# Attention and a layer of four experts on one core: rows of two groups loaded as 512-byte runs and regrouped, first weights in smaller parts, gate rows in steps, a new order

## The chip, the core and the metric

The kernel runs on one core of one Trainium2 chip. The metric is the device time of one execution in microseconds (us), and lower is better. The core has a matrix engine (TensorE, PE in the profile, with its weight loads as PEld), a vector engine (DVE), a scalar engine (ACT), a general engine (POOL) and one that issues transfers (SP). They work beside each other and wait for one another by semaphores. In this kernel POOL, SP and, for the first rows, ACT issue the transfers (DMAs).

## The reference

Sliding-window attention with four sink keys goes into a layer of four experts, whose outputs are mixed by normalized gates:

```python
batch, n_heads, seq, head_dim = (4, 8, 768, 64);  n_sink, window = (4, 128)
scores = scale * np.matmul(q, k.transpose(0, 1, 3, 2))
rel = pos[:, None] - pos[None, :]
keep = (pos[None, :] < n_sink) | ((rel >= 0) & (rel < window))
scores = np.where(keep, scores, -1000000000.0)
a = np.exp(scores - scores.max(-1)); a = a / (a.sum(-1) + 1e-09)
x = np.matmul(a, v)          # heads side by side: x is [3072, 512]
p = domain_probs / (domain_probs.sum(-1, keepdims=True) + 1e-09)
for e in range(4):           # w1[e] is [512, 1024], w2[e] is [1024, 512]
    h = np.maximum(x @ w1[e], 0.0)
    out += p[:, e:e + 1] * (h @ w2[e])
```

The inputs are fp32; the kernel computes in bf16 with fp32 sums.

## The kernel before, in words

**Tiling.** A batch has 768 tokens, taken as six row blocks of 128, and two row blocks are a *group* of 256 tokens (`g` is 0, 1, 2: groups one, two and three). Eight heads of 64 are four *head pairs* (`hp`) of 128 columns. For each group and head pair the kernel computes scores (L702), exponentials (ACT, L728, one for each of the two heads `ph`), the values product (L762 for the sink keys, L769 for the rest, with a column of ones that gives the denominator), the reciprocal (DVE, L796) and the normalized product, which is `x`, turned so that its columns lie on the partitions. For each group and expert there is then a first layer with w1 and a second layer with w2.

**Batch 0 differs from batches 1 to 3.** In batch 0 rows are loaded to SBUF and turned by TensorE (L596 in `transposes`, called a *flip*); the result lies in PSUM and is copied to `qkT` by ACT and DVE (L295 in `copy`; for group one two copies of 256 columns for a head pair, for the others one of 512 on either engine). Its `x` is normalized by DVE (L799) and turned by TensorE (L828, `turn`). In the other batches DMAs that transpose, issued by SP, do both (L270 in `turn_nat`, L786).

**The first rows.** `load_first` (L280) brings q and k of group one, half of the heads at a time, from SP's and ACT's queues in fp32, each partition with two neighbouring tokens, so that a run in DRAM is 512 bytes. `cast_first` (L301) turns them into bf16, one copy of 512 columns on DVE for q and one on ACT for k for each half. Groups two and three come by `load_nat` (L247): a DMA of 128 KB (in bf16) on POOL for each row block and each of q and k, which casts on the way; a run is one token of one head, 64 values, 256 bytes in DRAM and 128 bytes in SBUF.

**POOL's queue at the start.** In this order: values of row blocks 0 and 1 (`load_v`, L322), rows of group two (four loads), values of 2 and 3, w1 of expert 0 in two halves of its columns (`load_w1`, L332; 512 KB each as it lands in bf16), w2 of expert 0 as one (`load_w2`, L345; 1 MB). Behind it the loop issues the rows of group three (four loads), values of 4 and 5, then w1 and w2 of experts 1 and 2; w1 and w2 of expert 3 and all of batch 1 follow when the attention of batch 0 has been issued.

**Masks.** From an upper triangle made by a scan on DVE come two bias matrices `low` (two of the steps on ACT), and from these two masks (L543). In group one of batch 0 TensorE adds `low` to the scores by a product with the identity (L696); in the other groups of batch 0, and in all of batches 1 to 3, DVE multiplies the exponentials by the mask (L721, L737).

**First layer.** Two forms exist. The plain one (`hps`, L1081) makes four pairs of 128 hidden columns (`QF`), each 8 products of 256 columns, for one group and expert. The fast one (`cps`, L1169) does with seven half-size block products what takes eight otherwise; it needs sums of blocks of w1 (`vf`, DVE, L404 and its neighbours in `weight_form1`) and of `x` (`T`, DVE, L1138 in `tokens`), and DVE and ACT combine its results. If its second bank was last used by a tile that isn't a whole bank, one product of 512 columns sets the bank first (L1177). **Second layer.** In batch 0 it is plain (L1411): for each row block and expert 8 products of 512 columns, then a scaling by the gate into `osb` (ACT for expert 0, L1421, and DVE adds for the others, L1427). In batches 1 to 3 it is done by seven products too (`acc`, L1343), on sums of blocks of w2 (`wf`, `weight_form`).

**Gates.** For batch 0 the gates are turned by four small transposes (L931 in `gates`), just ahead of the first second-layer product. For the other batches `gates_by_row` (L457) normalizes all gate rows in four DVE steps (L458 to L462), SP writes them to DRAM, and `load_gate` (L479) spreads each over the partitions.

**Order.** There is no scheduler at run time: when the program is built, a planner walks along TensorE's clock. It keeps a modelled time for each engine and queue (`t`), for each load when it lands (`lands`, `sp`), and for each operand when it is ready. At every step it lists what TensorE could do next (an attention step, a product of the first layer, one of the second layer, one of `acc`), sorts by readiness and priority, and takes the first, or another where the table `OTHER` says so for that numbered choice. Work for ACT and DVE is put down by `later(engine, ready, slack, run)` and issued by `flush` when the modelled clock passes; "any" goes to the engine that is free sooner by the model. When nothing is ready early on, it issues idle products on zeros (`idle_products`, L572), 9 of 512 columns at the start and more of 256 where there is a gap. The numbers at the head of the function (`LOW_PRODUCT`, `DUE`, `MARGIN` and so on) weigh these choices.

Of the kernel before, what the change touches and what calls it, by code (L numbers as in the profile page):

```python
# [8 lines left out]
AF = mybir.ActivationFunctionType  # L9
# [7 lines left out]
def kernel(  # L17
# [12 lines left out]
    nc = tc.nc  # L30
# [28 lines left out]

    HELD = ("unit", "early")  # L60
    NGATE = 5
    ANYLAG = (-40.93, 0.0, 0.0, 51.99)
    OTHER = {31: 1, 83: 1, 70: 1, 73: 1, 106: 1, 189: 1, 149: 1, 182: 2, 132: 1, 90: 1, 164: 1, 318: 1, 197: 1, 569: 2, 56: 3, 61: 1, 12: 1, 62: 1, 5: 1, 15: 3, 71: 1, 84: 1, 107: 2, 165: 2, 151: 1, 95: 1, 86: 1, 173: 1, 152: 1, 155: 3, 279: 1, 235: 1, 266: 1, 316: 1, 381: 3, 379: 1, 194: 1, 343: 1, 283: 3, 273: 1, 325: 1, 328: 1, 267: 1, 482: 1, 499: 2, 571: 1, 396: 1, 564: 3, 496: 1}
    TOKENS0 = 0.0
# [3 lines left out]
    SHARE_OF = (1.034, 1.037, 1.072)  # L68
    LEAD = (1.027, 0.9932)
    DUE = (1.356, 1.635, 1.356, 1.356)  # L70
    LOW_PRODUCT = (2.147, 2.149, 2.147, 2.147)
    LOW_SECOND = (2.509, 2.509, 3.0, 2.509)
    HIGH_PRODUCT = -1
    EARLY = (0.1973, 0.1973, 0.1973, 0.1973)
    MASK_SLACK = (200.0, 984.1, 200.0, 200.0)
    GATE = (2639.0, 2639.0, 2639.0, 2639.0)
    GATE0 = (6000.0, 6000.0, 6000.0, 6000.0)
    FORM = (1000.0, 1000.0, 1000.0, 1000.0)
    TOKEN = (4927.0, 4559.0, 4924.0, 4559.0)
    MARGIN = (4621.0, 2117.0, 2117.0, 2117.0)  # L80
    HOLD = 0
    FULL = (8, 8, 9, 9)
    STEP0 = (0.2923, 0.1633, 0.2843, 0.2923)
# [12 lines left out]
    LOADN = 0  # L96
    BIASED = 1
# [8 lines left out]
    t = {"pe": 1200.0, "act": 0.0, "dve": 0.0, "pool": 1280.0, "sp": 800.0, "sw": 4800.0, "hw": 0.0}  # L106
# [5 lines left out]
    WARM = 6600.0  # L112
    FLIP, LATE = 103.6, 618.6
# [82 lines left out]
    ROW = {64: 12.8, 128: 22.6, 512: 79.8, 1024: 156.2}  # L196

    def lands(key, rows, cols, *deps):
        issued = pool(0, *deps, fixed=880)
        at = max(t["sw"], issued + 1500)  # L200
        t["sw"] = at + rows * ROW[cols] / 16
        landed[key] = t["sw"] + 900 + (BACKLOG if key[0] == "w1" or backed else 0.0)
        if key[0] == "w1":
            backed.append(key)
        moved.append([key, at, t["sw"], ROW[cols]])

    moved, backed = [], []
    BACKLOG = 1300.0
    TURNED, SHARE = 66, 31.0

    def sp(*deps, issue=530, takes=600, turning=False):
        t["sp"] = max([t["sp"], *deps]) + issue
        at = max(t["hw"], t["sp"] + 800)
        row = next((x[3] for x in moved if x[1] <= at < x[2]), 0.0)
        if turning and row:
            t["hw"] = at + TURNED * (row + SHARE)
            t["sw"] += TURNED * SHARE
            for x in moved:
                if x[2] > at:
                    x[1] += TURNED * SHARE * (x[1] > at)  # L220
                    x[2] += TURNED * SHARE
                    landed[x[0]] = x[2] + 900 + BACKLOG * bool(backed)
                    if x[0][0] == "w1" and ("w1", x[0][1]) in landed:
                        landed["w1", x[0][1]] = max(landed["w1", x[0][1]], landed[x[0]])
        else:
            t["hw"] = at + takes + max(0.0, min(takes, t["sw"] - at)) * (not turning)
        return t["hw"] + 900
# [38 lines left out]
    def turn_nat(b, tb):  # L266
# [7 lines left out]
        turned_at[b, tb] = sp(landed["qk", b, tb], scored_at.get(b - 1, 0.0), issue=1330, takes=1400, turning=True) + LATE  # L274
# [4 lines left out]

    def load_first():  # L280

        raw = {name: mo.tile([P, 2, 4, 2 * D], FP32, name=f"{name}raw", tag=f"wide{i}", bufs=1) for i, name in enumerate("qk")}
        for half in range(2):
            hs = slice(4 * half, 4 * half + 4)
            for name, src in (("q", q), ("k", k)):
                x = raw[name][:, half]
                (nc.sync if name == "q" else nc.scalar).dma_start(
                    out=x, in_=src[0, hs, 0:G, :].rearrange("h (p t) d -> p h (t d)", t=2),
                )
                nat[0, half, name, "raw"] = x  # L290
            landed["first", half] = ((4870.0, 5180.0), (7550.0, 7350.0))[half]
            t["sp"] += 530
# [4 lines left out]
    first = {name: sb.tile([P, 2, H, D], BF16, name="qkn", tag="qkn", bufs=NQB) for name in "qk"}  # L297
    qkn_free[-2:] = [1e12] * 2
    cast_at = {}

    def cast_first(half):  # L301
        hs = slice(4 * half, 4 * half + 4)

        def cast(at):
            cast_at[half] = at

        part = join(2, cast)
        for i, name in enumerate("qk"):
            def run(engine, i=i, name=name):
                copy(  # L310
                    engine, first[name][:, :, hs, :],
                    nat[0, half, name, "raw"].rearrange("p h (t d) -> p t h d", t=2),
                )
                part(clock(engine, 512))
            later(("dve", "act")[i], landed["first", half][i], 0, run)

    def rows_at(b, g):
        return max(landed.get(("qk", b, tb), 1e12) for tb in (2 * g, 2 * g + 1))
# [26 lines left out]
    def load_w2(e):  # L345
        w2_sb[e] = wpool.tile([P, NFB, Dout], BF16, name=f"w2_{e}", tag=f"w2_{e}")
        nc.gpsimd.dma_start(out=w2_sb[e], in_=moe_w2[e].rearrange("(fb p) d -> p fb d", p=P))
        lands(("w2", e), F, Dout)
# [104 lines left out]
    identf = scratch[:, 9 * P:10 * P]  # L453
    nc.sync.dma_start(out=dp, in_=moe_domain_probs.rearrange("(tb p) e -> tb p e", p=P))
# [3 lines left out]
    def gates_by_row():  # L458
        nc.vector.reduce_sum(out=ds, in_=dp, axis=AX.X)
        nc.vector.tensor_scalar_add(out=ds, in0=ds, scalar1=1e-9)  # L460
        nc.vector.reciprocal(out=ds, in_=ds)
        nc.vector.tensor_mul(  # L462
            pn, dp.rearrange("n p e -> n e p"), ds[:, None, :].to_broadcast([NT, E, P]),
        )
        for i in range(2):
            nc.sync.dma_start(out=gate_rows[:, :, i, :], in_=pn[i:NT:2])
        dve(1800, 0.0)

    gate_sb = {}

    def load_gates():

        while len(gate_sb) < len(mix.order) and (
            len(gate_sb) < NGATE or mix.order[len(gate_sb) - NGATE] in mix.finished
        ):
            b, g, e = mix.order[len(gate_sb)]
            load_gate(b * NG + g, e)

    def load_gate(pair, e):  # L479
# [6 lines left out]
        sp(takes=300)  # L486


    held = consts.tile([P, 2], BF16, name="held")
    nc.vector.memset(identf, 1.0)  # L490
    lent = wpool.tile([P, 12 * P], BF16, name="lent", tag=f"wf_{E - 2}")
    zeros = lent[:, 0:4 * P]
    nc.vector.memset(zeros, 0.0)
# [3 lines left out]
    for h in range(H):  # L497
        r = 32 * (h // 2) + NSINK * (h % 2)
        nc.sync.dma_start(
            out=vsf[r:r + NSINK, :, 0:D], in_=v[:, h, 0:NSINK, :].rearrange("b j d -> j b d"),  # L500
        )
    ident = consts.tile([P, P], BF16, name="ident")
    for sgn in (1, -1):
        nc.gpsimd.affine_select(
            out=identf, in_=identf, compare_op=ALU.is_ge, fill=0.0,
# [5 lines left out]
    t["sw"] += 500  # L511
    for tb in (2, 3):
        load_nat(0, tb)
    load_v(0, (2, 3))
    load_w1(0, 2, [0])
    load_w1(0, 2, [1])
    t["sw"] += 700
    load_w2(0)

    nc.vector.tensor_copy(out=ident, in_=identf)  # L520
    nc.vector.reduce_sum(
        out=sel2, in_=identf.rearrange("p (h x j) -> p h x j", h=NHP, j=NSINK)[:, :, 0:2], axis=AX.X,
    )
    own = lent[:, 4 * P:5 * P]
    nc.vector.tensor_tensor_scan(own, ident, ident, 0.0, ALU.add, ALU.max)
    two = own[:, None, :].to_broadcast([P, 2, P])
    LOW = 32768.0
    low = [lent[:, 5 * P:8 * P], lent[:, 8 * P:12 * P]]
    nc.vector.tensor_scalar(
        out=low[0].rearrange("p (n q) -> p n q", n=3)[:, 0::2], in0=two, scalar1=LOW, scalar2=-LOW, op0=ALU.mult, op1=ALU.add,  # L530
    )
    nc.vector.tensor_scalar(out=low[0][:, P:2 * P], in0=own, scalar1=-LOW, scalar2=None, op0=ALU.mult)
    nc.vector.memset(low[0][0:NSINK, 0:2 * P], 0.0)
    x = low[1].rearrange("p (n c q) -> p n c q", n=2, c=2)
    nc.scalar.activation(out=x[:, :, 0], in_=two, func=AF.Copy, scale=-LOW)
    nc.scalar.activation(out=x[:, :, 1], in_=two, func=AF.Copy, scale=LOW, bias=-LOW)
# [4 lines left out]
    def make_mask(i):  # L541
        def run(engine):
            x = (mask0, mask1)[i]  # L543
            nc.vector.tensor_scalar(out=x, in0=low[i], scalar1=1 / LOW, scalar2=1.0, op0=ALU.mult, op1=ALU.add)
            dve(4 * P)
            made.append(i)
        later("dve", 9500.0, 5000, run)

    for i in range(2):
        make_mask(i)  # L550
    t["dve"] = t["act"] = 4600.0
    cast_first(0)
    flush(4700.0)
    for x in vx:
        nc.vector.memset(x[:, :, D:DX], 1.0)
    t["dve"] += 240.0
# [10 lines left out]
    t["dve"] += 400.0  # L567
    cast_first(1)

# [1021 lines left out]
```

## Time and profile before

| | |
|---|---|
| time, median of 3 runs | 360.43 us (359.46 to 360.57) |
| the profiled execution, whole | 359.9 us |
| its span, first to last instruction | 358.0 us |
| TensorE busy, whole span | 350.0 us |
| DVE, ACT, POOL busy | 294.7, 169.0, 69.7 us |
| granted TensorE clock, mean | 1.00 |
| moved by DMAs | 37.25 MB, 104 GB/s on average |

The span begins with the first instruction and ends with the last; 1.9 us of the profiled execution lie outside it. Busy times of engines overlap and don't add up to the span. The page gives them for the whole span; the trace gives the same by stretches, by line of the kernel, by tile, and as waits, each with what ended it. In a row of such a view stand the start in us from the span's beginning, the length, engine, line, operation, and the operands as out<-in, with partitions x elements; `xN` is a count of neighbouring instructions of one kind, and what stands in brackets is idle time ahead and what ended it. "DMA share" is the mean busy share of the core's 16 DMA engines.

### The profile page before, as it was taken

Reading aid. Unit: us, or ns where it says so; the run is one execution under the profiler, and the core shown is the slowest. Engines: PE = TensorE matmul, PEld = TensorE weight load, DVE = VectorE, ACT = ScalarE, POOL = GpSimd, SP = SyncE. Lnnn points to the kernel's source line nnn. Section 1 sums busy time; section 2 is a strip of 40 time slices with the busy share of each in tenths; the row PEclk is TensorE's granted clock in tenths of the full one; section 3 lists DMA queues with packets and bytes.
Section 4 is the critical chain, followed back from the end, with each engine's and each line's share of the span. In section 5 each row is a group of like instructions: output and inputs, shape, how many; then the busy total and the mean of one; then the engine's idle time right before and its main releaser. Section 6 shows DMA issues by size and latency. Waiting matters only on the chain.

```text
span 358.0 us, 10605 instructions
## 1 busy us (share of the span) xinstructions
PE 350.0 (98%) x4457; PEld 296.5 (83%) x4470; DVE 294.7 (82%) x625; ACT 169.0 (47%) x425; POOL 69.7 (19%) x90
## 2 busy tenths in 40 slices
PE   8799999999999999999999999999999999999996
PEld 3484867766668888898999799899999999999985
DVE  6753999878948799899799789989989899897750
ACT  5775735557844555466455564655321313312110
POOL 8935116123910860010020000000000000000000
PEclk9999999999999999999999999999999999999999
DMA  9999999999999997618990141512102002100021
GB/s 172 182 187 200 210 210 176 147 145 174 154 169 214 173 178 66 99 47 101 168 160 19 32 79 42 60 60 60 34 16 90 26 22 78 29 31 31 2 73 46
DMA packets 117291, 37.25 MB, mean 104 GB/s; under 512 B 100612, under 2 KB 112740, under 8 KB 117244
## 3 DMA queue, kind: packets, MB, share of 16 engines
q0 software_dynamic: 77520, 17.31, 53.3%
q1 hardware_dynamic: 38668, 18.75, 26.4%
q8 instruction: 35, 0.57, 0.7%
q10 hardware_dynamic: 1056, 0.52, 0.6%
q14 instruction: 12, 0.10, 0.1%
HBM read 40.45 MB, written 9.49 MB: 139 GB/s over the span
## 4 chain that ended last, share of the span: by engine, by line
PE 83%; DMA 6%; DVE 4%; ACT 2%; POOL 2%; issue 2%; SPq 0%; DVEq 0%; POOLq 0%
PE cps L1169 32%; PE acc L1343 31%; PE acc L1411 8%; PE hps L1081 5%; DMA xT<-onat 2%; PE sps L702 2%; PE od L769 2%; DMA qkn<-in_k_dram 2%; DMA rows<-in_k_dram 1%; ACT aT L728 1%; DMA qkT<-rows 1%; DVE aT L721 1%; DVE osb L1427 1%; PE od L762 1%; POOL qkn L258 1%
## 5 line engine op out<-in xcount | busy, mean ns | idle before, releaser
L1169 PEld LDWEIGHTS <-w 128*128 128x128 bf16 x1248 | 77.3, 98 | 4.3 <-issue 2.0
L1343 PEld LDWEIGHTS <-H 128*128 128x128 bf16 x600 | 55.9, 98 | 5.9 <-issue 0.5
L1202 DVE SCALAR_TENSOR_TENSOR H<-cps,gates 128x512 bf16<-128x512 f32 x84 | 57.2, 684 | 3.1 <-PE cps L1169 1.3
L728 ACT ACTIVATE aT<-sps 128x512 bf16<-128x512 f32 (+1 forms) x96 | 47.2, 575 | 19.0 <-PE sps L702 18.9
L1169 PEld LDWEIGHTS <-vf 128*128 128x128 bf16 x768 | 47.5, 98 | 1.7 <-issue 0.2
L1343 PE MATMUL acc<-w,H 128*128 128x256 bf16 x360 | 48.8, 273 | 0.0
L1169 PE MATMUL cps<-T,w 128*128 128x128 bf16 x624 | 47.3, 219 | 0.2 <-DVE H L1237 0.2
L1169 PE MATMUL cps<-xT,w 128*128 128x128 bf16 x624 | 47.1, 219 | 0.0
L808 ACT ACTIVATE onat<-od,R 128x64 bf16<-128x64 f32 x144 | 33.5, 328 | 23.5 <-DVE R L796 23.3
L1411 PE MATMUL acc<-w,H 128*128 128x512 bf16 x179 | 43.4, 379 | 0.7 <-issue 0.2
L1215 ACT COPY cps<-cps 128x512 f32<-128x512 f32 x39 | 22.4, 577 | 43.4 <-PE cps L1169 40.1
L1169 PE MATMUL cps<-T,vf 128*128 128x128 bf16 x512 | 37.9, 219 | 0.0
L1081 PE MATMUL hps<-xT,w 128*128 128x256 bf16 x288 | 35.4, 273 | 0.1
L1411 PEld LDWEIGHTS <-H 128*128 128x128 bf16 x192 | 17.9, 98 | 17.7 <-issue 0.2
L324 POOL DMA_DIRECT2D vx<-in_v_dram x24 | 21.3, 896 | 55.3 <-PE od L769 50.1
L1081 PEld LDWEIGHTS <-w 128*128 128x128 bf16 x288 | 26.9, 98 | 3.8 <-issue 0.8
L1343 PEld LDWEIGHTS <-S 128*128 128x128 bf16 x288 | 27.0, 98 | 3.3 <-issue 0.5
L1222 DVE TENSOR_TENSOR cps<-H,cps 128x512 f32<-128x512 f32 x33 | 22.8, 692 | 6.9 <-PE cps L1169 5.6
L1237 DVE TENSOR_TENSOR H<-H,cps 128x512 f32<-128x512 f32 x33 | 22.6, 683 | 4.5 <-PE cps L1169 4.4
L1385 ACT COPY osb<-acc 128x256 f32<-128x256 f32 x28 | 10.5, 375 | 32.5 <-PE acc L1343 32.5
L1343 PE MATMUL acc<-wf,H 128*128 128x256 bf16 x184 | 24.8, 273 | 0.0
L1228 ACT COPY H<-cps 128x512 f32<-128x512 f32 x33 | 19.6, 593 | 10.7 <-PE cps L1169 10.7
(126 smaller groups left out, 543.8 us busy)
## 6 DMA issues: line engine op xcount, KB each, us to landing
w<-in_moe_w_dram POOLq DMA_DIRECT2D x7, 1024.0 KB, 16.8
out_dram<-osb SPq DMA_DIRECT2D x19, 256.0 KB
gates<-gate_rows SPq DMA_DIRECT2D x36, 128.0 KB
vx<-in_v_dram POOLq DMA_DIRECT2D x24, 128.0 KB, 7.9
rows<-in_q_dram POOLq DMA_DIRECT2D x12, 128.0 KB, 6.3
rows<-in_k_dram POOLq DMA_DIRECT2D x12, 128.0 KB, 6.8
qkn<-in_q_dram POOLq DMA_DIRECT2D x10, 128.0 KB, 13.9
qkn<-in_k_dram POOLq DMA_DIRECT2D x10, 128.0 KB, 13.3
```

Source lines behind the costliest of these rows:

```text
L324: nc.gpsimd.dma_start(out=vx[tb][:, :, 0:D], in_=v[b, :, tb * P:(tb + 1) * P, :].rearrange("h p d -> p h d"),)
L728: nc.scalar.activation(out=a[:, ph], in_=sps[ph][:, 0:w], func=AF.Exp, scale=scale)
L808: nc.scalar.mul(o[:, qi, hp, ph * D:(ph + 1) * D], od[:, qi, ph, 0:D], R[:, qi, ph])
L1081: nc.tensor.matmul(h[:, i].rearrange("p (q n) -> p q n", q=2), lhsT=w1_sb[e][:, db, fb * P:(fb + 1) * P], rhs=xT[b, g][:, :, db], start=(i ...
L1169: nc.tensor.matmul(y[:, f], lhsT=A[:, d, f * P:(f + 1) * P], rhs=T[:, d], start=(m in ("P1", "P5") and f == 0 and d == 0), stop=(d == 1), ...
L1202: nc.vector.scalar_tensor_tensor(out=dst, in0=src, scalar=0.0, in1=gate, op0=ALU.max, op1=ALU.mult)
L1215: nc.scalar.copy(out=tiles["Y"], in_=y)
L1222: nc.vector.tensor_add(tiles["V"], c5, tiles["X"])
L1228: nc.scalar.copy(out=c5, in_=y)
L1237: nc.vector.tensor_add(c5, c5, y)
L1343: nc.tensor.matmul(x, lhsT=self.operand(b, g, e, m)[:, f], rhs=forms[e][m][:, f], start=(k == 0 and f == 0 and m in (("P1", "P5", "P2") if ...
L1411: nc.tensor.matmul(op, lhsT=H[:, fb // QF, fb % QF, s], rhs=w2_sb[e][:, fb, :], start=(fb == 0), stop=(fb == NFB - 1),)
```

## The change

The reference's arithmetic is unchanged. The lines of the diff are those of the changed kernel; the planner's numbers are left out but for a few.

**Rows of groups two and three.** `load_runs(g)` takes the place of `load_nat(0, tb)`. One DMA brings q of the whole group and one brings k (256 KB each in bf16), in a layout with two neighbouring tokens side by side on a partition: a run is 512 bytes in DRAM and 256 bytes in SBUF. So that TensorE can turn them, each head pair is copied into the old layout (128 x 256 elements, DVE for q, ACT for k): 16 copies in all. The transposes then wait for the copies of their own head pair and not for whole row blocks, and the copy out of PSUM puts the two tokens back in order.

```python
def load_runs(g):
    x = mo.tile([P, 2, H, 2, D], BF16, name="runs", ...)
    for i, src in enumerate((q, k)):
        nc.gpsimd.dma_start(
            out=x[:, i].rearrange("p h t d -> p h (t d)"),
            in_=src[0, :, g * G:(g + 1) * G, :].rearrange("h (p t) d -> p h (t d)", t=2),
        )
...
    for hp in range(NHP):
        for i, engine in enumerate(("dve", "act")):
            def run(engine, i=i, h=2 * hp, part=part):
                copy(engine, rows[i][:, :, h:h + 2], x[:, i, h:h + 2].rearrange("p h t d -> p t h d"))
            later(engine, landed["qk", 0, g], 200 * hp, run)
```

**First rows.** The casts of group one are made for each head pair (256 columns each, four on DVE and four on ACT) in place of each half.

**First weights.** w1 of expert 0 comes in quarters of its columns, and a pair of hidden columns waits for its own quarter; w2 of expert 0 comes in two halves of its columns, so that its second layer is 8 products of 256 columns for each half, with a scaling for each:

```python
-    for tb in (2, 3):
-        load_nat(0, tb)
-    load_v(0, (2, 3))
-    load_w1(0, 2, [0])
-    load_w1(0, 2, [1])
+    load_runs(1)
+    if not VPOS:
+        load_v(0, (2, 3))
+    load_w1(0, QF, [0, 1])
...
+    load_w1(0, QF, [2, 3])
     t["sw"] += 700
     load_w2(0)
...
-        nc.gpsimd.dma_start(out=w2_sb[e], in_=moe_w2[e].rearrange("(fb p) d -> p fb d", p=P))
+        for c in halves(e):
+            nc.gpsimd.dma_start(
+                out=w2_sb[e][:, :, c], in_=moe_w2[e][:, c].rearrange("(fb p) d -> p fb d", p=P),
+            )
...
-            return max(free_at(), landed.get(("w1", e, 0), 1e12) if first else landed.get(("w1", e), 1e12), *xs)
+            return max(free_at(), landed.get(("w1", e, 0 if e else j), 1e12), *xs)
```

`emit_second` may now take any waiting second-layer product, the one that is ready first, and no longer only the oldest.

**Gate rows.** The four DVE steps of `gates_by_row` are put down one by one with a slack of 4 us each, and the SP transfers follow the last. They, and the loads behind them in the list (w1 and w2 of expert 3, rows and values of batch 1), are put down as soon as the list of loads is empty (`LOADN` = 1), and not when the attention of batch 0 has been issued.

```python
-    LOADN = 0
+    LOADN = 1
...
         if not loaded and (len(loads) < LOADN if LOADN else not att.more()):
             loaded = 1
             gates_by_row()
+            load_sinks(slice(1, B))
```

**Small work ahead of the rows.** The triangle is made by POOL's selections and a copy and not by a scan; only one bias matrix is kept, and the masks are made by three DVE steps; ACT's two steps go. The tile of zeros is 128x256 and not 128x512, and 13 idle products of 256 columns stand at the start in place of 9 of 512. The first rows of the values for the sink keys are loaded for batch 0 first (`load_sinks`, 8 small SP transfers), and for batches 1 to 3 by 8 more when the gate rows are put down.

**The planner.** The model of the queues (`lands`, `sp`), the weights at the head of the function and the table `OTHER` have new values, and with them TensorE's order is another from the first group on. In the changed program first-layer products of expert 0 stand between the attention steps of group three, eight at a time; the first products of experts 3 and 2 and the first scores of batch 1 stand earlier than before, counted in TensorE's work ahead of them, those of expert 3 by far the most. L1177 stands twice in the program, before once.

371 lines of the change are left out of this document (203 added, 168 removed).

## The prediction

> **What bounds the kernel now.** I read the page first, then TensorE's busy time by stretches, then its waits after 19 us.
>
> ```profile
> span 358.0 us, 10605 instructions
> PE 350.0 (98%) x4457; PEld 296.5 (83%) x4470; DVE 294.7 (82%) x625; ACT 169.0 (47%) x425; POOL 69.7 (19%) x90
> ```
> ```profile
> 5.60:18.15 12.55, 10.12 (x143) 1.00 1.95 180
> 18.15:26.43 8.28, 8.28 (x98) 1.00 1.67 188
> 26.43:340.00 313.57, 312.51 (x4079) 1.00 0.78 100
> 340.00:358.00 18.00, 14.88 (x137) 1.00 0.16 59
> ```
> ```profile
> PE acc L1411 <- issue: 0.2, 1, 0.2
> PE cps L1169 <- DVE H L1237: 0.2, 1, 0.2
> ```
>
> The columns of the second fence are stretch, length, TensorE's busy time with its instructions, granted clock, DMA share and GB/s. From 18.15 us on TensorE is full, at clock 1.00; the third fence is the whole list of its waits after 19 us, 0.4 us in sum. What is left there is its own work. So the change can gain only ahead of 18.15 us, where 143 matmuls take 12.55 us; and it can lose anywhere. The two anchors of my sum are the first expert product and the gate transposes (L931):
>
> ```profile
> 18.15 1.03 PE L1081 MATMUL hps<-xT,w 128*128 128x256 bf16 x8
> 26.43 0.65 PE L931 MATMUL acc<-scratch 24*128 24x24 f32 x4
> ```
>
> In the front the rows of group two and the values decide:
>
> ```profile
> 9.22 0.25 PE L769 MATMUL od<-vx,aT 128*128 128x65 bf16 x3 [0.18 <-DMA vx<-in_v_dram]
> 13.45 0.23 PE L596 MATMUL tr<-ident,qkn 128*128 128x128 bf16 x1 [1.04 <-DMA qkn<-in_k_dram]
> 19.74 0.76 POOL L337 DMA_DIRECT2D w<-in_moe_w_dram  x1 [1.09 <-DMA w<-in_moe_w_dram]
> ```
>
> The brackets name what ended the idle time. POOL's queue moves one load after another: the second values landed at 9.2, then four row loads, the last at 13.45, then two loads of values and the halves of w1, the second at 19.7.
>
> **The change, part by part.**
>
> *Ahead of the rows.* The casts in fours instead of twos, the masks without a scan and without ACT's two steps, the smaller zero tile, the sink loads of one batch: all of it is done before the k rows of group two land (below), and TensorE waits for these rows; that wait hides it. If group one's chain ended later than the landing, each us of it would count.
>
> *Rows of group two.* Two loads of 256 KB take the place of four of 128 KB; the bytes are the same, so the gain is the packet rate (and two POOL issues, which lie ahead of the queue and gain nothing).
>
> ```profile
> 7.00:10.00 3.00, 2.52 (x26) 1.19 (x25) 2.01 (x6) 2.66 (x7) 3.00 (x5) 1.00 2.41 155
> 16.00:22.00 6.00, 5.60 (x90) 4.67 (x90) 5.56 (x19) 5.00 (x13) 3.41 (x5) 1.00 1.25 208
> 0.91 0.17 DVE L490 MEMSET scratch<- 128x128 f32 x1 [0.91 <-PEq L1572]
> ```
>
> The last number of a stretch is GB/s: 155 while rows and values with 128-byte pieces in SBUF move, 208 while the w1 halves and w2 with 1024-byte pieces do. The new pieces have 256 bytes. 256 KB take 1.69 us at 155 GB/s and 1.26 us at 208; per packet the two rows are 13.2 and 78.8 ns on each of 16 engines, a line between them gives 22.6 ns at 256 bytes, and so 1.45 us, which I take (nearer to the slow row). Before, four loads took 4.23 us where their bytes take 3.38, so 0.21 us a load is added. POOL starts later by one memset of DVE, at most 0.17 us; I take 0.15. The k rows then land at 9.22 + 0.15 + 2 x (1.45 + 0.21) = **12.7 us**; bounds 11.9 (208 GB/s, nothing added) and 13.6 (155 GB/s, all 0.85 added).
>
> The Trainium skill, "DMA: Bandwidth & Descriptors", Specifications, says that transfers reach line rate, about 27 GiB/s an engine, from 512 bytes on. The source runs are now 512 bytes; an estimate by that page is 17.7 ns a packet, 1.13 us a load, and rows at about 12.0. No row here has such packets beside a cast.
>
> *Regrouping.* New are 16 copies of 128x256, eight on DVE and eight on ACT. Group two's four k copies stand in ACT's queue with one exponential of the last head pair of group one between them.
>
> ```profile
> 6.02 0.65 ACT L295 COPY qkT<-tr 128x256 bf16<-128x256 bf16 x2 [0.42 <-PE tr L596]
> 10.10 1.76 ACT L728 ACTIVATE aT<-sps 128x384 bf16<-128x384 f32 x4 [0.44 <-PE sps L702]
> 13.77 1.07 ACT L295 COPY qkT<-tr 128x512 bf16<-128x512 bf16 x2 [1.91 <-issue]
> ```
>
> One copy of 256 takes 0.37 us alone and each further one 0.28 (the rows' two in 0.65); one more exponential of 384 takes 0.42. Four copies and one exponential are 1.6 us after landing: 14.3. Behind that exponential wait, in TensorE's order, the values of that head pair and then all 16 transposes of group two; they lie inside the 1.6 us. Then ACT does two of the four PSUM copies (1.07, to 15.4) and DVE the others. The scores of the first two head pairs start when the first of each are done, at 14.9. The q copies on DVE come from the load that lands first, and are hidden under ACT's; without that cover they cost up to 4 x 0.28 us.
>
> *w1 in quarters.* The first quarter, 256 KB in 512-byte pieces (1.3 us by the same line), lands two value loads (2 x 0.85) and 1.3 us after the k rows, 15.7; by the 19.7 us row the weights came 0.4 us sooner than such a sum, so 15.3 to 15.7. Before, the whole half was needed. It is not the last to come: after 12 score matmuls the first expert product starts at
>
> ```profile
> 15.97 0.29 PE L663 MATMUL sinks<-qkT,ksd 128*32 128x256 bf16 x4
> 16.19 0.84 PE L702 MATMUL sps<-qkT 64*128 64x128 bf16 x12
> 17.42 0.23 PE L762 MATMUL od<-vsd,sinkA 128*128 128x130 bf16 x1 [0.39 <-ACT sinkA L671]
> 21.91 0.23 PE tx L828 x4
> 22.13 4.37 PE hps L1081 x40
> 9.51 0.18 DVE L796 RECIPROCAL R<-od 128x4 f32<-128x4 f32 x1 [0.48 <-PE od L769]
> 9.73 0.42 DVE L799 TENSOR_TENSOR onat<-od,R 128x256 bf16<-128x256 f32 x1
> ```
>
> 14.9 + 0.84 = 15.75 us. From there to the gate transposes the changed order has 32 products (0.109 each by the chain's 4.37/40: 3.5), sinks (15.97 to 16.19: 0.2), 12 more score matmuls (0.84), 40 value matmuls with sinks (20 from 17.42 to 18.15: 1.46) and 8 transposes (0.46): 6.45 us. In it the transposes wait for DVE's reciprocal and product (9.51 to 10.15: 0.64 us after the values, in part under other values); bounds 0 and 0.8, I take 0.2, since 10 to 20 other value matmuls lie between. Gate transposes: 15.75 + 6.45 + 0.2 = 22.4. Before, 64 products stood ahead of them, now 32; the 32 still to do are 3.5 us, so 25.9 compares with 26.43: **-0.5 us**.
>
> *w2 in halves* and one more setting product (L1177 stands twice in the program, before once):
>
> ```profile
> 31.54 1.74 PE acc L1411 x8
> 128.64 0.87 PE acc L1343 x8
> ```
>
> 48 products of 512 columns become 96 of 256: 96 x 0.109 - 48 x 0.217 = +0.05 us. L1177's 512 columns cost +0.2. The first half lands at 12.7 + 2 x 0.85 + 4 x 1.3 + 2.65 (512 KB by the same line) = 22.3, before the first second-layer product, 0.6 behind the gate transposes at 23.0. Twelve ACT scalings of 256 take the place of six; ACT is half idle.
>
> *Gate rows in four steps, earlier.*
>
> ```profile
> 40.96 0.66 DVE L459 TENSOR_REDUCE scratch<-scratch 24x128 f32<-24x512 f32 x1
> 41.66 0.21 DVE L460 TENSOR_SCALAR scratch<-scratch 24x128 f32<-24x128 f32 x1
> 41.90 0.94 DVE L461 RECIPROCAL scratch<-scratch 24x128 f32<-24x128 f32 x1
> 42.88 1.08 DVE L462 TENSOR_TENSOR scratch<-scratch 24x512 f32<-24x512 f32 x1
> 23.00:28.00 5.00, 4.95 (x41) 3.94 (x40) 1.47 (x6) 2.99 (x5) 2.59 (x4) 1.00 2.31 160
> 40.00:50.00 10.00, 9.95 (x92) 7.55 (x91) 9.69 (x20) 4.85 (x9) 1.75 (x2) 1.00 1.18 209
> 50.00:60.00 10.00, 9.89 (x111) 7.17 (x111) 9.63 (x17) 4.06 (x7) 4.84 (x6) 1.00 1.79 181
> ```
>
> 2.9 us of DVE go from 41 to 44 us, where it is 97% busy (the third number with its count), to the time around the gate transposes, where it is 29% busy. SP issues eight more small sink loads and the gate loads earlier; its row transposes, one for each row block, keep their count. I cost it at nothing, because TensorE did not wait at 41 us either.
>
> *Group three's rows, the new order.* They are loads ahead of w1 of expert one, which before was waited for by nobody. Over the whole program the matmuls are the same but for the two terms above and filling products. The order from 30 us on is new; TensorE's later waits (0.4) can go to 0 or grow; I take no change, bounds -0.4 and +1.5.
>
> Sum: -0.5 + 0.05 + 0.2 = about **-0.3 us**: span 357.7. The profiled execution took 359.9 with a span of 358.0; the median of the runs shown is 360.43 (359.46 to 360.57), half a microsecond above it. On the median's scale the forecast is **360.1 us**.
>
> **The rivals.**
>
> *Rows land at once* (faster). If the 256-byte pieces move at the weights' 208 GB/s, the k rows land at 11.9, 0.8 us sooner, the w1 quarter with them, and all behind it, to the gate transposes, follows one for one, since ACT's and TensorE's chain hangs on it: -1.1 us; with the later 0.4 us gone too, -1.5. I take 359.1. For it: packets of 512 bytes at the source are twice those of the 155 GB/s row. Against: the line between the rows. The page's line rate named above leads to nearly this time.
>
> *DVE becomes the bound at 40 to 60 us* (slower). It is busy 19.3 of 20 us there.
>
> ```profile
> L404 DVE TENSOR_TENSOR vf<-vf,w 128x1024 bf16<-128x1024 bf16 x3 | 2.1, 690 | 0.1
> L1138 DVE TENSOR_TENSOR T<-xT 128x512 bf16<-128x512 bf16 x12 | 5.0, 419 | 2.8 <-DMA xT<-onat 2.7
> L1138 DVE TENSOR_TENSOR T<-xT,T 128x256 bf16<-128x256 bf16 x24 | 6.8, 284 | 0.3
> ```
>
> In the changed order the first product on a form of expert two's w1 stands 3.8 us of TensorE's work sooner (the matmuls ahead of it, counted at the intervals above), so four forms of 0.69 (2.8 us) are due sooner. The token differences of groups one and two (0.42 + 2 x 0.28 each, 2 us) have moved from the front to behind group three's transposes. Against that stand the gate rows' 2.9 us that left. It decides when more than the 0.7 us that DVE has free there is added net; 2.6 of the 4.8 would make TensorE wait 1.9: -0.3 + 1.9 = +1.6, **362.0 us**. Against it: TensorE passed this stretch with two waits of 0.2.
>
> *The change does nothing for the rows*: at 155 GB/s with the added lag they land at 13.6, and the regrouping eats the rest: +0.6 us, 361.0; still within the bound of the forecast.
>
> **How the numbers follow.** A measurement of this kernel can tell about 0.3%, 1.1 us, from no change. The forecast, near 360.1 with its own range 359.4 to 361.4 (rows between 12.0 and 13.6), has 0.46, the rows that land unchanged included. Rows at once 0.34, DVE 0.20. So faster 0.34, within 0.46, slower 0.20. The range reaches from 358.5, the fast rival and some of the unread order, to 361.8, most of the slow one; 0.2 is left out.
>
> **What would show it.** The first transposes of group two near 13.5 us, the first expert product near 15.8 and the gate transposes near 22.4, then a list of TensorE's waits no longer than now: right. k rows at or under 12.0, or over 13.6: the load's price was wrong. TensorE waiting for DVE between 40 and 60 us: the slow rival. Waits later than that, or a product that waits for w1 of expert three, which now has its first one far earlier: nothing in my sum covers it.

## The result

The changed kernel takes 359.50 us (median of 20 runs, 359.35 to 359.88); the kernel before, run beside it, takes 360.40 (20 runs, 359.46 to 361.40). The ratio is 0.9982, 95% interval 0.9975 to 0.9989. The profiled execution of the changed kernel took 359.52 us with a span of 357.8.

Two things stand side by side here. The median fell by 0.9 us, and the spread fell from 1.94 to 0.53 us; but the two profiled executions differ by only 0.2 us in span. The experiments show that these are two effects. About half of the executions of before did not run at full clock (the clocks of the 20 above are not on record; of 87 others, run beside the experiments, 45 had a mean granted clock of 0.994 or 0.995). Their median is 360.41 us, that of the other 42 is 359.72. So most of the median's gain is the clock, and about 0.2 us is left for the order itself, as in the two profiles.

### The profile page after: what moved, and what is told of

Same layout as the page of the kernel before. It is cut to its first block, busy times and chain, and to the rows that moved or that the text cites. A ratio compares the mean times of both kernels' runs of the same rounds, so it can differ in the third digit from the quotient of the medians.

```text
span 357.8 us, 10767 instructions
## 1 busy us (share of the span) xinstructions
PE 350.9 (98%) x4525; PEld 302.6 (85%) x4534; DVE 296.2 (83%) x635; ACT 172.1 (48%) x440; POOL 69.0 (19%) x89
## 4 chain that ended last, share of the span: by engine, by line
PE 94%; DVE 2%; DMA 2%; ACT 1%; issue 0%; ACTq 0%
PE cps L1202 34%; PE acc L1376 31%; PE acc L1453 12%; PE hps L1114 8%; PE sps L738 3%; PE od L805 3%; DMA raw<-in_k_dram 2%; DVE aT L773 1%; PE od L798 1%; DVE onat L835 1%; PE tx L864 0%; ACT aT L764 0%; PE sinks L699 0%; DVE H L1129 0%; PE tr L632 0%
## 5 line engine op out<-in xcount | busy, mean ns | idle before, releaser
L1376 PEld LDWEIGHTS <-H 128*128 128x128 bf16 x600 | 55.1, 98 | 7.3 <-issue 2.0
L1235 DVE SCALAR_TENSOR_TENSOR H<-cps,gates 128x512 bf16<-128x512 f32 x84 | 56.4, 681 | 1.5 <-PE cps L1202 0.7
L1453 PE MATMUL acc<-w,H 128*128 128x512 bf16 (+1 forms) x231 | 45.2, 335 | 0.5
L1453 PEld LDWEIGHTS <-H 128*128 128x128 bf16 x240 | 22.5, 98 | 14.3 <-issue 0.3
L1376 PE MATMUL acc<-wf,H 128*128 128x256 bf16 x176 | 23.7, 273 | 0.0
```

The source lines that it names most:

```text
L1235: nc.vector.scalar_tensor_tensor(out=dst, in0=src, scalar=0.0, in1=gate, op0=ALU.max, op1=ALU.mult)
L1376: nc.tensor.matmul(x, lhsT=self.operand(b, g, e, m)[:, f], rhs=forms[e][m][:, f], start=(k == 0 and f == 0 and m in (("P1", "P5", "P2") if ...
L1453: nc.tensor.matmul(op, lhsT=H[:, fb // QF, fb % QF, s], rhs=w2_sb[e][:, fb, c], start=(fb == 0), stop=(fb == NFB - 1),)
```

## The profile after

The head of the page, then TensorE by the same stretches as before (stretch, length, busy time with its instructions, granted clock, DMA share, GB/s), then all of TensorE's waits after 19 us:

```profile
span 357.8 us, 10767 instructions
PE 350.9 (98%) x4525; PEld 302.6 (85%) x4534; DVE 296.2 (83%) x635; ACT 172.1 (48%) x440; POOL 69.0 (19%) x89
```
```profile
5.60:18.15 12.55, 11.71 (x143) 1.00 1.80 185
18.15:26.43 8.28, 7.61 (x98) 1.00 1.60 191
26.43:340.00 313.57, 313.09 (x4139) 1.00 0.78 100
340.00:358.00 18.00, 14.33 (x132) 1.00 0.17 60
```
```profile
PE hps L1114 <- DMA w<-in_moe_w_dram: 0.6, 1, 0.6
```

TensorE is busier up to 18.15 us (11.71 us against 10.12; part of it are idle products) and less busy in the next stretch, where before it was full: a wait for w1 has moved there. Behind that the list has no wait left. The anchors of the prediction, from the time order of ACT and TensorE:

```profile
11.68 0.40 ACT L296 COPY qkn<-runs 128x256 bf16<-128x256 bf16 x1
12.80 0.84 PE L632 MATMUL tr<-ident,qkn 128*128 128x128 bf16 x12
15.11 1.05 PE L1114 MATMUL hps<-xT,w 128*128 128x256 bf16 x8 [0.34 <-DMA w<-in_moe_w_dram]
18.78 1.05 PE L1114 MATMUL hps<-xT,w 128*128 128x256 bf16 x8 [0.58 <-DMA w<-in_moe_w_dram]
22.85 0.65 PE L966 MATMUL acc<-scratch 24*128 24x24 f32 x4
```

ACT copies the first k rows of group two at 11.68 us, so they have landed (13.45 before). Group two's transposes start at 12.80, the first expert product at 15.11 (18.15 before, with other work ahead of it). Then the third pair of hidden columns waits 0.58 us for its quarter of w1, and the gate transposes come at 22.85. With the 32 products still to do, 3.5 us, that compares with 26.43: a gain of 0.1 us where the prediction had 0.5.

How fast the runs of group two move stands in a row over half a microsecond of their transfer. The columns are the busy times of PE, PEld, DVE, ACT and POOL, then clock, DMA share and GB/s:

```profile
9.50:10.00 0.50, 0.42 (x10) 0.43 (x11) 0.47 (x2) 0.50 (x3) 0.50 (x2) 1.00 1.82 181
```

From the gate transposes to the last copy of the output, the two profiles give:

```profile
354.92 0.37 ACT L1385 COPY osb<-acc 128x256 f32<-128x256 f32 x1 [4.87 <-PE acc L1343]
```
```profile
354.36 0.37 ACT L1418 COPY osb<-acc 128x256 f32<-128x256 f32 x1 [4.87 <-PE acc L1376]
```

Before it is 354.92 - 26.43 = 328.49 us, after 354.36 - 22.85 - 3.5 = 328.0, so 0.5 less. But behind that copy the changed kernel needs 357.8 - 354.36 = 3.44 us, the one before 358.0 - 354.92 = 3.08. The sum is -0.1 - 0.5 + 0.36 = -0.2 us, the difference of the spans. The median's 0.9 us isn't in these two profiles at all.

## Experiments on the changed kernel: what sets its front

In these seven the order on TensorE is that of the changed kernel, instruction for instruction, and so are ACT's and DVE's, save for the copies that two of them have no use for; the planner counts the loads where they stood, and only their issue is changed. Times are medians. The kernel before was run beside them in three groups, with medians of 360.27, 359.97 and 360.14 us (360.40 beside the changed kernel). "Gate" is the start of the gate transposes (22.85 in the changed kernel).

**Values behind three quarters of w1.**

```python
-    if not VPOS:
-        load_v(0, (2, 3))
-    load_w1(0, QF, [0, 1])
-    if VPOS:
-        load_v(0, (2, 3))
-    load_w1(0, QF, [2, 3])
+    load_v(0, (2, 3), send=False)
+    load_w1(0, QF, [0, 1, 2])
+    for tb in (2, 3):
+        send_v(0, tb)
+    load_w1(0, QF, [3])
```

With `send=False` the planner counts the two loads where they stood; `send_v` issues them.

> The changed kernel with the two loads of values 2 and 3 moved behind the third quarter of w1 in POOL's queue; the order on TensorE, ACT and DVE is the same. In the changed kernel TensorE waits 0.34 us for the first quarter (to 15.11 us) and 0.58 for the third (to 18.78), while the values, landed at 13.69, are used from 19.66 on. Theory 'weights' (the queue of loads sets the front): both waits go, the values land near 18.6 before they are used, the gate transposes move from 22.85 to about 22.0, time 358.6 us (359.5 - 0.9). Rival 'chain' (scores, exponentials, masks set it, and the waits for w1 only fill time in which TensorE would wait anyway): the first product moves, but the values stay at 19.5 to 19.7 and the gate transposes at 22.6 to 22.9; time 359.3 to 359.5.

Measured: 360.11 us (ratio to before 0.9995, 0.9986 to 1.0004), 0.6 more than the changed kernel, gate at 23.02. Neither theory had this. The profiled execution is one of the two shortest of the eleven (359.75 us, span 358.0): it shows 0.2 of the 0.6, the gate's 0.17; where the other 0.4 lies is not shown. The waits for w1 are gone, and another one stands in their place. TensorE's first wait in the list, then POOL in order of time:

```profile
PE sinks L702 <- POOL ksd L665: 0.6, 1, 0.6
```
```profile
15.16 0.88 POOL L317 DMA_DIRECT2D runs<-in_k_dram  x1 [0.75 <-DMA w<-in_moe_w_dram]
16.06 0.89 POOL L665 TENSOR_TENSOR ksd<-qkT,half 128x8 bf16<-128x8 bf16 x4
```

POOL's products for the sink keys (`ksd`) stand behind a load whose issue waits for an earlier load's landing: with the values put back, that earlier load is a quarter of w1, and it lands later. In the changed kernel too POOL gets to the keys only at 14.86 us; there the wait for w1 and the first eight products stand ahead of the sink scores at 16.09, which wait for nothing.

**The same, and the keys ahead of group three's loads.** POOL issues `ksd` and `vsd` first, then the two loads of rows.

```python
-        for i, src in enumerate((q, k)):
+        def send(i, src):
             nc.gpsimd.dma_start(...)
+        for i, src in enumerate((q, k)):
+            if g == 1:
+                send(i, src)
+            else:
+                behind_keys.append((send, i, src))
...
                     sink_keys(b)
                     sink_values(b)
+                    for send, i, src in behind_keys:
+                        send(i, src)
```

> The run with the values behind the third quarter of w1, and POOL's products for the sink keys and sink values (L662, L677 of the changed kernel) put ahead of its loads of the rows of group three. In the run before, TensorE waited 0.6 us for the sink keys, which stood in POOL's queue behind a load whose issue waited for the landing of an earlier load. Theory 'POOL's queue': with the keys ahead of it no wait for w1 or the keys is left, the gate transposes come at 22.0 (changed kernel 22.85), time 358.6 to 358.8. Rival 'chain': the exponentials and masks of group two end no sooner, a wait for them takes the place, gate transposes at 22.6 or later, time 359.3 or more.

Measured: **358.67 us** (358.56 to 359.01; 6 runs; ratio to before 0.9963, 0.9951 to 0.9976), the fastest of all. POOL and TensorE in order of time:

```profile
12.74 0.67 POOL L670 TENSOR_TENSOR ksd<-qkT,half 128x8 bf16<-128x8 bf16 x4
```
```profile
17.66 1.05 PE L1125 MATMUL hps<-xT,w 128*128 128x256 bf16 x8
21.97 0.66 PE L977 MATMUL acc<-scratch 24*128 24x24 f32 x4
```

The keys come 3.3 us sooner than in the run before this one, the third pair waits for nothing, the gate moves by 0.88 us against the changed kernel, the span by 0.8 (357.8 to 357.0) and the median by 0.83 (0.7 by the ratios to before): "POOL's queue" holds, and the end follows the front one for one.

**The keys alone.** The second edit without the first.

> The changed kernel with only the sink keys and values on POOL put ahead of its loads of the rows of group three; the values' loads stay ahead of w1. Theory 'both are needed': TensorE still waits 0.34 and 0.58 us for w1, gate transposes near 22.85 us, time 359.4 to 359.6. Rival 'keys alone': POOL's products no longer run beside DVE's masks at 15.5 us (one took 1.56 us there), the values start sooner, time under 359.2.

Measured: 359.52 us, gate at 23.05; TensorE still waits 0.9 us for w1. Both edits are needed.

**w1 in halves.**

```python
-            nc.gpsimd.dma_start(out=w1_sb[e][:, :, i * n:(i + 1) * n], ...)
+            m = n if e else 2 * n
+            if e or i % 2 == 0:
+                nc.gpsimd.dma_start(out=w1_sb[e][:, :, i * n:i * n + m], ...)
```

> The changed kernel with w1 of expert 0 in two halves, as before, and nothing else moved. Theory 'weights': the first product waits until the first half is there, 16.6 us in place of 15.1, the third until the second half is there, 19.8 in place of 18.8; the gate transposes come 1.0 us later, near 23.9, time 360.5. Rival 'chain': the values at 19.7 move by 0.3 at most, time 359.5 to 359.8.

**w2 whole.** One load of 1 MB in `load_w2`; the products stay at 256 columns.

> The changed kernel with w2 of expert 0 as one load of 1 MB, its products still of 256 columns and in the same order. Theory 'weights': the load lands at 25.1 us or later, the first second-layer product, at 23.44 now, waits for it 1.7 us, and that stays to the end: 361.2. Rival: the wait is got back behind it, since loads that follow aren't late and TensorE's later small waits shrink: under 360.2.

Measured: w1 in halves 360.24 us with the gate at 23.47, w2 whole 360.93. Each has one wait at the load in question, from the list of waits of the one and of the other:

```profile
PE hps L1116 <- DMA w<-in_moe_w_dram: 1.5, 1, 1.5
```
```profile
PE acc L1451 <- DMA w<-in_moe_w_dram: 1.3, 1, 1.3
```

Both theories "weights" hold in kind and were sized too high (1.0 and 1.7 us expected, 0.74 and 1.43 measured). So in this order the quarters are worth 0.7 us and the halves of w2 1.4.

**Rows straight into the transposes' layout.**

```python
-                out=x[:, i].rearrange("p h t d -> p h (t d)"),
-                in_=...rearrange("h (p t) d -> p h (t d)", t=2),
+                out=rows[i][:, tt], in_=...rearrange("h (p t) d -> t p h d", t=2)[tt],   # four loads, no copies
```

> The changed kernel with the rows of groups two and three loaded straight into the layout of the transposes, four loads of 128 KB with 128-byte pieces in SBUF as before, and no regrouping copies; the order is the same. Theory 'weights': the rows take 4.2 us in place of 2.7, and all loads behind them come 1.5 us later; the third quarter of w1 lands at 20.2, the gate transposes come near 24.3, time 361.0. Rival 'chain': the transposes of group two wait for the rows to 13.4 in place of 12.8, and the rest follows by that 0.6 us; the copies' time on ACT and DVE is got back; time 359.9 to 360.1.

Measured: 363.85 us, outside both. POOL in order of time, and TensorE's first wait:

```profile
17.87 0.89 POOL L318 DMA_DIRECT2D qkn<-in_k_dram  x1 [0.81 <-DVE aT L772]
18.77 0.67 POOL L661 TENSOR_TENSOR ksd<-qkT,half 128x8 bf16<-128x8 bf16 x4
```
```profile
PE sinks L698 <- POOL ksd L661: 2.3, 1, 2.3
```

Again the keys, now behind four loads of rows and not two; the last of these waits 0.81 us, by the view for DVE and not for a landing. The profiled execution (362.17 us) is the only one of the six at full clock: its gate comes at 25.52, 2.7 us later than in the changed kernel, and its time is 2.7 longer. The other five had a mean clock of 0.991 to 0.995 and took 363.29 to 365.10, so the rest of the median's 4.35 us goes with the fallen clock. To price the loads themselves, the same edit was made on the fastest version:

> The fastest version so far (values behind the third quarter of w1, keys ahead of the rows of group three; 358.67 us) with the rows of groups two and three loaded straight into the transposes' layout, in 128-byte pieces, without regrouping copies. So POOL's queue holds no more work behind waiting loads, and what is left is the price of the loads themselves. Theory 'load time': rows land at 13.1 us, 1.5 later than as runs, w1 and the values follow 1.5 later each, the values product near 19.7 in place of 18.9 and more waits for w1: time 359.6 to 360.2. Rival 'copies cost as much': the transposes start at 13.1 in place of 12.9, ACT and DVE are free of 16 copies, time 358.6 to 359.1.

Measured: 359.18 us (358.89 to 361.16), 0.5 over the fastest version, between the two theories; gate at 21.94, not later than with runs. What it loses comes behind it: TensorE waits 0.46 us for w2, and three of the twelve executions, the profiled one among them, are 1 us and more longer, at a clock of 0.999 or 1.00 (the profiled one waits 1.6 us for the sinks of batch 1). So the 512-byte runs are worth 0.5 us here, and 2.7 us at full clock where they keep POOL's queue short.

## Experiments on the kernel before: where the median's gain comes from

**Before, once more,** and with one part of the change each: the gate rows early (the four DVE steps moved into `gates`), and the rows as runs with their copies (`load_runs` in the old order).

> The kernel before, unchanged, as a second look at its spread: its runs went from 359.46 to 361.40 us, those of the changed kernel from 359.35 to 359.88, and its profiled execution (359.9) lies in its lower part. Theory 'front': in a longer execution the added time lies ahead of 27 us (a load that lands later), and from the gate transposes to the end it takes the same 328.5 us as in the first profile. Rival 'spread': the added time lies behind 27 us, in many small waits. The profile decides if this execution is longer than the first by 0.3 us or more.

> The kernel before with one part alone: the four DVE steps of the gate rows (2.9 us) issued right behind the gate transposes, near 27 us, and not at 41 us; SP's transfers of them and all else stay where they are. Theory 'DVE decides at 40 to 50 us': DVE's queue is 2.9 us shorter there, TensorE's losses between 30 and 50 us (0.4 us more than in the changed kernel) go, time 360.0. Rival 'TensorE does not wait for it': 360.3 to 360.5, as the prediction has it.

> The kernel before with one part of the change alone: the rows of groups two and three as 512-byte runs in two loads each and regrouped by 16 copies; the order on TensorE is that of before, w1 stays in halves and w2 whole. Theory 'rows pay by themselves': k rows at 11.6 us in place of 13.4, transposes of group two at 12.9 in place of 13.45, first expert product at 17.5 (18.15), gate transposes at 25.8 (26.43); time 359.8, 0.6 under before. Rival 'rows need the new order': exponentials and masks stand behind the copies on ACT and DVE, the first expert product stays at 18.0 to 18.6; time 360.2 to 360.8.

Measured: 359.98, 359.68 (ratio 0.9992, 0.9983 to 1.0002) and 362.03 us; the last two each lie outside both theories. The first is what matters: its profiled execution took 360.53 us with a mean clock of 0.995. TensorE there by stretches (busy time, clock, DMA share, GB/s):

```profile
10.00:11.60 1.60, 1.60 (x25) 1.00 2.49 154
11.60:13.50 1.90, 0.29 (x3) 1.00 2.45 161
13.50:16.90 3.40, 3.39 (x35) 0.50 1.28 205
```

While it waits for the rows, TensorE is busy for 0.29 of 1.90 us; then the granted clock is 0.50 for 3.4 us. In the first profile of before, with 0.35 of 1.90 us busy just ahead of it, the same stretch had a clock of 1.00:

```profile
13.50:16.90 3.40, 3.39 (x54) 1.00 1.27 204
```

In the slower execution the gate transposes come late by it, and the rest takes its usual time:

```profile
27.55 0.65 PE L931 MATMUL acc<-scratch 24*128 24x24 f32 x4
...
355.62 0.37 ACT L1385 COPY osb<-acc 128x256 f32<-128x256 f32 x1 [4.87 <-PE acc L1343]
```

That is 328.1 us from gate to last copy, so theory "front" holds, with another cause than a late load. Of the twelve executions six had a mean clock of 0.994 or 0.995 and took 360.13 to 361.14 us; the other six had 1.00 and took 359.28 to 359.82. The latter are near the changed kernel's times (359.35 to 359.88). Among the 87 executions run beside the experiments the two groups overlap: 359.97 to 361.02 us with a fallen clock, 359.29 to 360.44 without.

The run with early gate rows has the same 328.1 us (26.36 to 354.47), and at a clock of 0.999 or more 359.43 to 359.88: nothing is gained by them alone. Its median is under both of its theories as only 2 of its 11 executions had a fallen clock (of before, run beside it, 11 of 23). It also shows that 0.3 of the first profile's 328.5 us was one wait, absent here and in the other profiled execution of before. The first profile has it at the line below; the products from there on start 0.45 us later than in this run, those ahead of it 0.14:

```profile
112.92 0.61 PE L1169 MATMUL cps<-T,w 128*128 128x128 bf16 x8 [0.16 <-DVE H L1237]
```

The rows as runs in the old order cost 2 us, 1.6 against those executions of before that had a fallen clock too (median 360.38): TensorE waits 1.09 and 0.65 us, from 10.4 us on, for copies out of PSUM that stand behind the regrouping, and the clock fell in all six executions (0.51 from 13.5 to 16.9 us in the profiled one).

```profile
PE sps L735 <- DVE qkT L331: 1.1, 1, 1.1
PE sps L735 <- ACT qkT L331: 0.7, 1, 0.7
```

Where the 16 copies stand in ACT's and DVE's queues was my choice there, so this says that the runs need an order made for them, not what they would cost in the best one.

**Idle products in the wait.**

```python
                 rows = first["qk"[i]]... if (b, g) == (0, 0) else nat[b, 2 * g + tt][:, i, hs]
+                if (b, g, hp) == (0, 1, 0) and tt:
+                    for _ in range(4 + 4 * i):
+                        nc.tensor.matmul(acc[1][:, 0:G], lhsT=zeros[:, 0:P], rhs=zeros[:, 0:G], start=True, stop=True)
```

> The kernel before with 12 idle products of 256 columns put on TensorE between the first four transposes of group two, 4 while it waits for the q rows and 8 while it waits for the k rows; all else is unchanged. In the second look at the kernel before, the granted clock fell to 0.50 from 13.5 to 16.9 us in the profiled execution, and 6 of its 12 executions had a mean clock of 0.994 or 0.995 and took 360.1 to 361.1 us, the other 6 a clock of 1.00 and 359.3 to 359.8. Theory 'clock' (the wait for the rows lets the clock fall, and the changed kernel's gain in the median is that it doesn't): all executions have a clock of 0.998 or more, the median is 359.5 and the highest under 360. Rival 'order': the clock falls as often, or the idle products cost what they save; median 360.0 to 360.4 with the old spread.

Measured: 359.64 us, 359.32 to 359.88, ratio to before 0.9983 (0.9975 to 0.9992), clock 0.998 or more in all 11 executions. By stretches:

```profile
11.60:13.50 1.90, 1.35 (x14) 1.00 2.48 161
13.50:16.90 3.40, 3.39 (x55) 1.00 1.28 206
```

Twelve products on zeros bring the gain of the change in the median, to within 0.14 us (359.64 against 359.50; by the ratios to before 0.9983 against 0.9982). Theory "clock" holds.

**The changed kernel without its eight idle products there.**

```python
+            idles += 1
+            if 11 < idles < 20:
+                pe(G)
+            else:
+                idle_products(spare[-1], 1, G)
-            idle_products(spare[-1], 1, G)
```

> The changed kernel without the eight idle products that stand ahead of group two's transposes (between 11.75 and 12.6 us); all else is unchanged. Theory 'clock': some of the executions show a mean clock of 0.995, these take 360.1 us or more, and the median rises to between 359.6 and 360.5. Rival: its rows come soon enough that the clock does not fall without them, all executions at 359.3 to 359.9.

Measured: 359.50 us, 359.38 to 359.60, clock 0.998 or more in all 11. The rival holds:

```profile
11.60:13.50 1.90, 1.27 (x21) 1.00 1.95 174
```

With its rows sooner the changed kernel keeps TensorE busy for 1.27 of these 1.90 us by its own work. In this order rows that come 1.8 us sooner are enough, in the old one idle products are; in the old order with the runs, where TensorE waited for the copies instead, the clock fell.

## Why the prediction was right, and where its steps were not

The forecast was 360.1 us, -0.3 on the median's scale, with no change beyond 0.3% the likeliest outcome (0.46); measured are 359.5, -0.65 us by the ratio and -0.9 by the medians. It lies in the range, 0.1 us above the lower end of the forecast's own 359.4. In the spans the sum is close, 357.8 for 357.7, but by other terms than its own: that its errors cancel there is luck, and most of the median's gain is no term of it.

- **Bound.** Right: the work behind the front is full, the end follows the gate transposes one for one (gate to last copy, the 32 moved products taken off: 328.0 us in the changed kernel, and 353.50 - 21.97 - 3.5 = 328.0 in the fastest version).
- **Rows of group two.** Mis-sized: landed by 11.68 us, not at 12.7, under the lower bound of 11.9. The price of the packets was right. At 181 GB/s, as the profile after has it while the runs move, 256 KB take 1.45 us, just what the prediction took. What did not come is the 0.21 us added for each load, and the later start: by the trace's landings the second values were there at 8.9 us (the sum has 9.37) and the two row loads 2.7 us behind them. The rival "rows at once" had the landing right, but not by its own reason, the 208 GB/s, and it was wrong that all behind it "follows one for one".
- **w1 in quarters.** The step that failed. The prediction said of the first quarter that it "is not the last to come" and looked at no other. The first was waited for, 0.34 us, and the third 0.58; the front gave 0.1 us and not 0.5. From the first product to the gate transposes the changed kernel takes 7.74 us where the sum has 6.65: the wait for the third quarter is 0.58 of it. The other 0.5 is there in the fastest version too, which has no wait for w1 (14.80 to 21.97, 7.17 us), and was not taken apart.
- **w2 in halves, the setting product.** Costed at +0.25 us; gate to end gained 0.1 against the typical 328.1 of before. What in the new order pays for the difference was not taken apart.
- **Gate rows, and DVE as the bound.** Right at nothing; the slow rival did not come, the list has no wait for DVE behind 19 us.
- **The end.** Not in the sum: 0.36 us more from the last copy to the end of the span. It is there in all nine profiles with the changed order (3.44 to 3.50 us) and in none of the five with the old one (3.03 to 3.08). By the trace's landings it lies behind the last output's landing (1.35 us to the end of the span, 0.98 before). Its cause is open.
- **The clock.** Not in the prediction at all, and it is most of the median's gain. The sign was there: the profiled execution lay half a microsecond under the median, and I took this for an offset of the scale. The clock of 1.00 in its rows was that of the better half of the executions.

The Trainium skill, "TensorE: Matmul & The Clock Gate", Part 1, says that the clock is halved after at least one idle window of about 3.4 us and is back after about 3.4 us of sustained work, and that the window runs free of the kernel. The trace agrees with the half and with the 3.4 us until it is back (13.5 to 16.9 us), and the runs with the chance in it (6 of 12 executions); it doesn't agree with the length of the idle time, which was 1.9 us here, with 0.29 of it busy.

## What to carry to other kernels

Where the runs of a kernel fall into two groups, a profile shows one of them: compare the granted clock of the executions before an average is explained. Work put behind loads on the queue that issues them waits for landings that aren't its own. When a load gets faster, look for the next one in the same queue, all its parts and not the first alone.

## What the runs showed of the hardware

The clock fell by chance, and on the whole more often after longer waits. Executions with a mean clock of 0.995 or less, with the longest wait of TensorE in the profile:

| kernel | longest wait, us | clock fell |
|---|---|---|
| changed kernel | 0.6 | 0 of 20 |
| keys alone | 0.8 | 0 of 12 |
| w2 whole | 1.3 | 2 of 12 |
| w1 in halves | 1.5 | 1 of 11 |
| before, with early gate rows | 1.3 idle of 1.9 | 2 of 11 |
| before | 1.6 idle of 1.9 | 6 of 12, and 45 of 87 beside the experiments |
| before with runs | 1.7 idle of 2.1 | 6 of 6 |
| rows straight | 2.3 | 5 of 6 |
| rows straight on the fastest version | 1.6, in the profiled execution | 0 of 12 |

The last row shows that a wait of 1.6 us does not always do it. Where the clock fell was seen in two profiles alone, before (run once more) and before with runs; that it fell at the longest wait in the others is likely and not shown.

A fall costs 0.7 us in the medians of before (360.41 against 359.72), 1.8 us in w2 whole (362.65 against 360.89) and 2.4 in w1 in halves (362.59 against 360.24). One stretch of 3.4 us at half the clock can cost 1.7 us where TensorE is full, so the 2.4 holds something more; those executions have no profile.

A mask on DVE took 1.56 us in the changed kernel where another took 0.41; POOL's product for the sink values ran at the time. With that product earlier the same two masks take 0.91 us (DVE after, POOL after, DVE with the keys first):

```profile
15.27 1.90 DVE L773 TENSOR_TENSOR aT<-aT,mask 128x512 bf16<-128x512 bf16 x2 [0.23 <-ACT aT L764]
```
```profile
15.50 1.05 POOL L677 TENSOR_TENSOR vsd<-vsf,sel 128x520 bf16<-128x520 f32 x1
```
```profile
15.67 0.91 DVE L778 TENSOR_TENSOR aT<-aT,mask 128x512 bf16<-128x512 bf16 x2 [0.23 <-ACT aT L769]
```

The times of the two runs are the same (359.52 against 359.50), and that POOL's product is the cause wasn't tested by itself.
